# One core, three chained layers: a second PSUM tile for the last stage, its first block inside the last unit, and its rows loaded earlier

## The chip, the core and the metric

The kernel runs on one core of a Trainium2 chip. The core's engines each run their own list of instructions in order and wait for each other through semaphores: TensorE (PE in the profile, with PEld for its weight loads), VectorE (DVE), ScalarE (ACT), GpSimd (POOL), and SyncE (SP), which here issues nearly all DMA transfers. The metric is the time of one execution on the device in microseconds (us). Three runs of the kernel before took 1320.35, 1321.07 and 1323.45 us; the median is 1321.07.

## What is computed

The reference chains three layers over 4608 tokens of 512 numbers (batch 8, 8 heads, 576 positions, 64 per head). Cut to what matters:

```python
# 1. linear attention with random features
phi(x) = concat(exp(x @ w_phi - m), exp(-(x @ w_phi - m))),  m = max|x @ w_phi|
x = (phi(q) @ (phi(k).T @ v)) / (phi(q) @ sum(phi(k)))
# 2. mixture of 8 experts: each token goes to the expert with the largest logit
logits = x @ w_gate + modality_bias[modality_id]
out[mask_e] = gate_w * (relu(x[mask_e] @ w1[e]) @ w2[e])     # 512 -> 1024 -> 512
# 3. dense layer with a SoLU
h = x @ w_in                                                  # 512 -> 1024
solu = h * softmax(h)
ln = (solu - mean) / sqrt(var + 1e-6) * g_ln
result = ln @ w_out                                           # 1024 -> 512
```

## The kernel before

Products are made in a format that rounds, so each operand is split into a high and a low part and each product is three matmuls: high by high, high by low, low by high. `mm3` (L1071) issues the three, and its line, L1074, stands at almost every matmul below.

*Attention* fills the first 440 us; the change does not touch it. At its end the tokens lie in HBM (`xe`), sorted by expert.

*The experts* follow as units. Unit 0 has 128 rows; units 1 to 17 have 256 each (pairs); unit 18, the last (NU - 1), has 128 again; then come four *minis* of 32 rows, each of another expert. A pair unit runs `mm1` (four blocks of 24 matmuls of 256 columns, each block into one PSUM tile `tp`, read by ScalarE, L1088, and VectorE, L1089, in `relu_split`), in the midst of it eight transposes for the next unit's rows (`xT`, L898), and `mm2` (96 matmuls). The tile `tp` comes from the pool `bank` of 6 PSUM banks (L964). In `mm2` of a pair unit the two halves of the output have a `tp` each; half 0 is complete after step 2 of 4, half 1 after step 3, and each is copied (`yo`, L1188) and sent to HBM (`yd`, L1152) when it is complete. For the single unit 18 `mm1` keeps rows on partitions, so its result is turned by eight transposes (`tr_single`, L1108), which is put off in the list `mids` and run by `run_mids`. Weights come through eight buffers (ldk, ldq, ldv in the trace) that SP fills again as soon as they have been split; in unit 18 it fills them with weights of the minis.

The minis are a generator, `quad` (L1341): each `next(minis)` does one step of it (load rows; transpose; four steps of 32 small matmuls at L1357; transpose; four steps at L1373; copy; transpose and four stores to `yd`, L1386). 

*The last stage* works on 36 tiles of 128 tokens. `load_y(j)` loads two tiles' rows from `yd` into the SBUF buffer `yin` (L1210). Its address in `yd` is fixed, but units store at addresses held in registers, so it waits until every store issued before it has landed. `yT(i)` (L1216) splits a tile into high (`yTh`, ScalarE, L925) and low (`yTl`, GpSimd, L926). `a3(i)` (L1234) makes `h` by 24 matmuls of 512 columns into one PSUM tile of two banks (named `h2` in the code, `h` in the profile; pool `hps`, one buffer, L965), then the softmax and the norm: two maxima (DVE, L1244), the exponential (ACT, L1249), the product (DVE, L1254, the last that reads `h`), the centring (DVE, L1256), the squares (ACT, L1259). `turn` (L1224) has VectorE transpose the result in blocks of 32 (L1226) and sends it through HBM (`turned`, L1228, and `wlo`, L1232) to finish the transpose; `lnT` (L1272) splits what comes back (ACT L1281, DVE L1282); `a4(i)` (L1285) is the second product, 24 matmuls of 512 columns, and stores the rows.

`block()` (L1459) puts these together: in block n it issues `yT(n+1)`, `load_y` where n is even, `a3(n)`, `lnT(n-2)` and `a4(n-3)`. So the first three blocks have an `a3` and no `a4`. The order of issue is the order of the code on PE; after the units the other engines' orders come from a scheduler that follows the code closely. `units` (L1482) issues `load_y(0)` just before unit 18, but after the stores of unit 17, and `yT(0)` after unit 18. In unit 18 (L1405) the first two steps of the minis that use PE are issued between `mm1` and `mm2`. After the units, L1499 alternates one step of the minis with two blocks.

Of the kernel before, what the change touches and what calls it, by code (L numbers as in the profile page):

```python
# [17 lines left out]
P = 128  # L18
# [936 lines left out]
def moe(ctx, m):  # L955
# [5 lines left out]
    p2 = ctx.enter_context(tc.tile_pool(name="m_2", bufs=2, reuse_waits="tile"))  # L961
    p1 = ctx.enter_context(tc.tile_pool(name="m_1", bufs=1, reuse_waits="tile"))
    wp = ctx.enter_context(tc.tile_pool(name="m_w", bufs=1, reuse_waits="tile"))
    bank = ctx.enter_context(tc.tile_pool(name="m_b", bufs=6, space=PSUM, reuse_waits="tile"))  # L964
    hps = ctx.enter_context(tc.tile_pool(name="m_h", bufs=1, space=PSUM, reuse_waits="tile"))  # L965
    KD, KF = DM // P, DFF // P
    NU = 2 + NUNIT
    m.rp, m.xin = rp, p1
# [5 lines left out]
    def weights():  # L974
        gl = p1.tile([P, KF], F32, name="gl")
        SP.dma_start(out=gl, in_=m.g_ln.rearrange("(c p) -> p c", p=P))
        n = 2 * KD + KF
        tiles = {}

        def load(i):  # L980
            if i < 2 * KD:
                rows, c0 = m.w_in[(i // 2) * P : (i // 2 + 1) * P, :], (i % 2) * 512
            else:
                rows, c0 = m.w_out[(i - 2 * KD) * P : (i - 2 * KD + 1) * P, :], 0
            tiles[i] = p1.tile([P, 512, 2], I32, name=("yin", "ex")[i % 2])
            SP.dma_start(out=tiles[i], in_=rows[:, c0 : c0 + 512].bitcast(I32).rearrange("p (n two) -> p n two", two=2))

        load(0)
        yield
        for i in range(n):  # L990
            if i + 1 < n:
                load(i + 1)
            src = tiles.pop(i)
            h, l = src[:, :, 1], src[:, :, 0]
            ab = p1.tile([P, 2, 512], I32, name="wab")
            a, b = ab[:, 0, :], ab[:, 1, :]
            V.tensor_scalar(out=a, in0=h, scalar1=3, scalar2=0x3FFFFFF8, op0=ALU.logical_shift_left, op1=ALU.bitwise_and)
            V.scalar_tensor_tensor(out=b, in0=h, scalar=-0x40000000, in1=a, op0=ALU.bitwise_and, op1=ALU.bitwise_or)
            yield
            V.tensor_scalar(out=a, in0=b, scalar1=-0x800000, scalar2=None, op0=ALU.bitwise_and)  # L1000
            V.tensor_scalar(out=l, in0=l, scalar1=9, scalar2=None, op0=ALU.logical_shift_right)
            yield
            a, b = a.bitcast(F32), b.bitcast(F32)
            V.scalar_tensor_tensor(out=a, in0=l, scalar=2.0**-43, in1=a, op0=ALU.mult, op1=ALU.mult)
            V.tensor_tensor(out=a, in0=a, in1=b, op=ALU.add)
            V.tensor_scalar(out=h, in0=h, scalar1=0x7FF00000, scalar2=None, op0=ALU.bitwise_and)
            yield
            V.scalar_tensor_tensor(out=b, in0=h, scalar=float(897 << 20), in1=a, op0=ALU.is_ge, op1=ALU.mult)
            if i < 2 * KD:
                hi, lo = [t[:, (i % 2) * 512 : (i % 2 + 1) * 512] for t in win[i // 2]]  # L1010
                m.split(b, hi, lo, V)
            else:
                f = i - 2 * KD
                hi, lo = [t[:, f % 2, :] for t in wout[f // 2]]
                A.mul(hi, b, gl[:, f : f + 1])
                V.scalar_tensor_tensor(
                    out=lo, in0=b, scalar=gl[:, f : f + 1], in1=hi.bitcast(F32), op0=ALU.mult, op1=ALU.subtract
                )
            yield
# [70 lines left out]
        return hi, lo  # L1090

    def tr(src, nms, pool):
        hi, lo = [pool.tile([P, DFF], F32R, name=nm).rearrange("p (k t) -> p k t", k=KF) for nm in nms]
        for b0 in range(0, KF, 4):
            tp = bank.tile([P, 4, P], F32, name="tp")
            for j in range(4):
                T.transpose(tp[:, j, :], src[:, (b0 + j) * P : (b0 + j + 1) * P], c.ident)
            m.evac(hi[:, b0 : b0 + 4, :], lo[:, b0 : b0 + 4, :], tp)
        return hi, lo
# [50 lines left out]
    def put(o, u, n, dc):  # L1150
        rows = yd[dc * P : (dc + 4 // n) * P, m.cols(u)]
        SP.dma_start(out=rows.rearrange("(c p) t -> p c t", p=P), in_=o)  # L1152
# [15 lines left out]
    def mm2(us):  # L1168
        acc = {}
        for j in range(4):  # L1170
            fh, dh = j // 2, j % 2
            ch = (us[-1], 4 + j)
            w = chunks.pop(ch)
            for u in us:
                h = hT[u]
                if m.size(u) == 2:
                    if fh == 0:
                        acc[u, dh] = bank.tile([P, 2, 2 * P], F32, name="tp")
                    o = acc[u, dh]
                    for dc in range(2):  # L1180
                        for f in range(4):
                            mm3(
                                o[:, dc, :], both(w, lambda t: t[:, f, dc * P : (dc + 1) * P]), h(4 * fh + f),
                                fh == dc == f == 0, fh == 1 and f == 3,
                            )
                    if fh == 1:
                        yo = p2.tile([P, 2, 2 * P], F32, name="yo")
                        A.copy(yo, o)  # L1188
                        put(yo, u, 2, 2 * dh)
                else:  # L1190
                    if j == 0:
                        acc[u] = bank.tile([P, 2, 2 * P], F32, name="tp")
                    o = acc[u]
                    for f in range(4):
                        mm3(o[:, dh, :], h(4 * fh + f), both(w, lambda t: t[:, f, :]), j == f == 0, fh == 1 and f == 3)
                    if j == 3:
                        put_rows(o, u)
            used(ch)
            yield
        slots[0] += sum(m.size(u) for u in us)  # L1200
# [5 lines left out]
    def load_y(j):  # L1206
        assert 2 * j + 2 <= slots[0] - (NEW + 2 * NPAIR + NSING + 1 - NT), (j, slots)
        c0 = YCOLS - 2 * P * (j + 1)
        t = p1.tile([P, 4, 2 * P], F32, name="yin")
        SP.dma_start(out=t, in_=yd[:, c0 : c0 + 2 * P].rearrange("(c p) t -> p c t", p=P))  # L1210
        g = p2.tile([P, 2, 2], F32, name="gt", bufs=5)
        SP.dma_start(out=g, in_=gd[c0 : c0 + 2 * P, :].rearrange("(t p) w -> p t w", p=P))
        for n in range(2):
            ys[2 * j + n] = (t[:, :, (1 - n) * P : (2 - n) * P], g[:, 1 - n, 0:1], g[:, 1 - n, 1:2])
# [17 lines left out]
            SP.dma_start(out=lv[g], in_=dv[g])  # L1232

    def a3(i):  # L1234
        h = hps.tile([P, DFF], F32, name="h2")
        y = yt.pop(i)
        sc = lambda nm: p2.tile([P, 1], F32, name="s_" + nm)
        halves = [slice(n * 512, (n + 1) * 512) for n in range(2)]
# [69 lines left out]
    def extra(j):  # L1308
# [2 lines left out]
        e, xo = regs[u][:2]  # L1311
        for i in range(8):
            m.load_raw(i, e)
        x = p1.tile([P, DFF], F32, name="yin")[:, 0:DM]
        SP.dma_start(out=x, in_=m.xe[bass.ds(xo, P), 0:DM])
        m.keep_gates(u)

# [23 lines left out]
    def quad():  # L1341
# [40 lines left out]
        A.copy(yr, b.rearrange("p a d -> p (a d)"))  # L1382
        yield
        yo = blocks(yr, KD, [p2.tile([P, 4, P], F32, name="yo")])[0]
        for g, u in enumerate(us):
            SP.dma_start(  # L1386
                out=yd[:, m.cols(u)].rearrange("(c p) t -> p c t", p=P), in_=yo[:, :, group(g)]
            )
        slots[0] += 1
        yield  # L1390

    def run(g):
# [12 lines left out]
    def unit(u):  # L1405
        gap(u)
        g = mm1(u)
        for i in range(4):
            next(g)
            if i == XAT:  # L1410
                run_mids()
                next_x(u)
                if u == NU - 2:
                    next(minis)
        run(g)
        gap(u)
        if u == NU - 1:
            next(minis)
        run_mids()
        if u == NU - 1:  # L1420
            next(minis)
        run(mm2([u]))

    with ExitStack() as sp:
# [30 lines left out]
    mids.extend(held)  # L1455
    ctx.enter_context(tc.manual_schedule(engines={mybir.EngineType.SP}))
    nxt = [0, 0, 0]

    def block():  # L1459
        n, split, done4 = nxt  # L1460
        run_mids()
        if n + 1 < NT:
            yT(n + 1)
            if n % 2 == 0 and n + 2 < NT:
                load_y((n + 2) // 2)
        if n == NT - 1:
            lnT(split)
        if n < NT:
            a3(n)
            nxt[0] += 1  # L1470
        if split < n - 1:
            if n < NT - 1:
                lnT(split)
            nxt[1] += 1
        if done4 < n - 2:
            a4(done4)
            nxt[2] += 1
# [4 lines left out]

    def units(u0, u1):
        for u in range(u0, u1):
            if u == START - 1:
                run(bg)
                load_y(0)
            unit(u)
            if u == START - 1:
                yT(0)  # L1490

    minis = quad()
    with tc.manual_schedule(engines=MANUAL):
# [2 lines left out]
    if ENDMAN:  # L1496
        ctx.enter_context(tc.manual_schedule(engines=MANUAL))
    with tc.manual_schedule(engines=QMAN):
        for _ in minis:  # L1499
            block()  # L1500
            block()
# [76 lines left out]
```

## Time and profile before

| | us |
|---|---|
| median of three runs | 1321.07 |
| the profiled execution | 1319.59 |
| its span on the core | 1317.5 |
| PE busy in the span | 1270.6 (96%) |
| granted TensorE clock, mean | 0.988 |
| the last matmul ends, from the span's start | 1302.86 |

The span goes from the first instruction to the last; 2.1 us of the execution lie around it. The profile lists for each engine the groups of instructions with their busy time, and for each wait what ended it. A matmul of 512 columns is shown as 0.39 us long, but matmuls are pipelined and one starts every 0.23 us; the length of a run of them is read from the chain of waits, which merges them. [...]

### The profile page before, as it was taken

Reading aid. Unit: us, or ns where it says so; the run is one execution under the profiler, and the core shown is the slowest. Engines: PE = TensorE matmul, PEld = TensorE weight load, DVE = VectorE, ACT = ScalarE, POOL = GpSimd, SP = SyncE. Lnnn points to the kernel's source line nnn. Section 1 sums busy time; section 2 is a strip of 40 time slices with the busy share of each in tenths; the row PEclk is TensorE's granted clock in tenths of the full one; section 3 lists DMA queues with packets and bytes.
Section 4 is the critical chain, followed back from the end, with each engine's and each line's share of the span. In section 5 each row is a group of like instructions: output and inputs, shape, how many; then the busy total and the mean of one; then the engine's idle time right before and its main releaser. Section 6 shows DMA issues by size and latency. Waiting matters only on the chain.

```text
span 1317.5 us, 25489 instructions
## 1 busy us (share of the span) xinstructions
PE 1270.6 (96%) x9242; PEld 1064.4 (81%) x9242; DVE 865.9 (66%) x1620; ACT 668.2 (51%) x1254; POOL 409.8 (31%) x479
## 2 busy tenths in 40 slices
PE   8999999999999989999999999987999998999997
PEld 6777777777775989999999999855877787888885
DVE  7758867866885758777877878625555554555561
ACT  5666666666664345554555555513333443444442
POOL 6655665674672100000000000012233233333331
PEclk9999999999999999999999999988999998999998
DMA  8712421241132232215322221786767555556552
GB/s 241 209 53 64 132 96 57 92 143 49 50 130 81 74 91 67 79 59 171 94 81 66 81 81 26 231 258 166 200 188 202 137 132 131 139 131 151 136 136 56
DMA packets 273762, 156.81 MB, mean 119 GB/s; under 512 B 181824, under 2 KB 255712, under 8 KB 273632
## 3 DMA queue, kind: packets, MB, share of 16 engines
q1 hardware_dynamic: 267648, 136.01, 37.9%
q0 software_dynamic: 5824, 19.04, 3.8%
q8 instruction: 76, 1.25, 0.4%
q14 instruction: 54, 0.44, 0.1%
q10 hardware_dynamic: 160, 0.07, 0.0%
HBM read 166.67 MB, written 51.37 MB: 165 GB/s over the span
## 4 chain that ended last, share of the span: by engine, by line
PE 56%; DMA 3%; DVE 2%; issue 1%; ACT 1%; SPq 1%; POOLq 0%; ACTq 0%; DVEq 0%
PE tp L1074 39%; PE h L1074 14%; DMA yd<-yo 2%; PE tp L898 1%; DMA ldv<-in_moe_w_dram 1%; PE tp L1373 1%; ACT ex L1249 0%; DVE ex L1254 0%; DVE wlo L926 0%; PE tp L1357 0%; DMA yin<-yd 0%; SPq L1232 0%; DVE s_mx L1244 0%; DMA out_dram<-wab,gt 0%; DMA turned<-whi 0%
## 5 line engine op out<-in xcount | busy, mean ns | idle before, releaser
L322 POOL TENSOR_TENSOR es<-es,e 128x512 f32<-128x512 f32 x128 | 164.0, 1288 | 102.0 <-ACT e L278 90.4
L926 POOL TENSOR_TENSOR yTl<-yin,yTh 128x512 fp32r<-128x512 f32 x36 | 46.9, 1302 | 451.3 <-ACT yTh L925 447.6
L1244 DVE TENSOR_REDUCE s_mx<-h 128x1 f32<-128x512 f32 x72 | 46.4, 687 | 125.4 <-PE h L1074 125.4
L1074 PE MATMUL tp<-xTh,whi 128*128 128x256 f32 x432 | 122.4, 283 | 2.4 <-PEq L1443 2.4
L1074 PE MATMUL tp<-xTh,wlo 128*128 128x256 f32 x432 | 121.5, 281 | 0.0
L1074 PE MATMUL tp<-xTl,whi 128*128 128x256 f32 x432 | 121.3, 281 | 0.0
L1074 PE MATMUL tp<-hTl,whi 128*128 128x256 f32 x432 | 119.7, 277 | 0.4 <-DVE hTl L1089 0.4
L1074 PE MATMUL tp<-hTh,wlo 128*128 128x256 f32 x432 | 119.6, 277 | 0.3 <-DVE wlo L926 0.3
L1074 PE MATMUL tp<-hTh,whi 128*128 128x256 f32 x432 | 119.5, 277 | 0.0
L1249 ACT ACTIVATE ex<-h,s_mx,gt 128x1024 f32<-128x1024 f32 x36 | 43.4, 1207 | 136.0 <-issue 78.3
L271 DVE TENSOR_REDUCE m<-mm 128x4 f32<-128x512 f32 x144 | 97.1, 680 | 15.9 <-PE mm L269 15.9
L259 DVE TENSOR_TENSOR lo<-tp,hi 128x512 fp32r<-128x512 f32 x72 | 49.5, 687 | 81.8 <-ACT hi L258 81.3
L267 PE MATMUL mm<-wphi_hi,hi 128*128 128x256 f32 x288 | 93.8, 326 | 1.1 <-ACT hi L258 1.1
L1259 ACT ACTIVATE sq<-ex 128x1024 bf16<-128x1024 f32 x36 | 38.1, 1058 | 97.8 <-DVE ex L1256 97.8
L1262 POOL TENSOR_SCALAR rs<-s_var,gt 128x1 f32<-128x1 f32 x36 | 12.4, 344 | 236.3 <-ACT sq L1259 236.3
L1074 PEld LDWEIGHTS tp<-xTh,whi 128*128 128x128 f32 x432 | 82.1, 190 | 2.6 <-ACTq L1443 2.6
L338 ACT ACTIVATE qp<-tp 128x512 f32<-128x512 f32 x128 | 69.4, 597 | 25.8 <-PE tp L330 22.7
L1074 PEld LDWEIGHTS tp<-xTl,whi 128*128 128x128 f32 x432 | 81.9, 190 | 0.0
L1074 PEld LDWEIGHTS tp<-xTh,wlo 128*128 128x128 f32 x432 | 81.9, 190 | 0.0
L1074 PEld LDWEIGHTS tp<-hTl,whi 128*128 128x128 f32 x432 | 81.1, 188 | 0.6 <-DVE hTl L1089 0.6
L1074 PEld LDWEIGHTS tp<-hTh,wlo 128*128 128x128 f32 x432 | 81.1, 188 | 0.5 <-DVE wlo L926 0.5
L1074 PEld LDWEIGHTS tp<-hTh,whi 128*128 128x128 f32 x432 | 81.2, 188 | 0.0
(427 smaller groups left out, 3904.9 us busy)
## 6 DMA issues: line engine op xcount, KB each, us to landing
ldk<-in_moe_w_dram SPq DMA_DIRECT2D x66, 512.0 KB
ldv<-in_moe_w_dram SPq DMA_DIRECT2D x66, 512.0 KB
ldq<-in_moe_w_dram SPq DMA_DIRECT2D x44, 512.0 KB
turned<-whi SPq DMA_DIRECT2D x35, 512.0 KB
wlo<-turned SPq DMA_DIRECT2D x140, 128.0 KB
yd<-yo SPq DMA_DIRECT2D x36, 256.0 KB
yin<-yd SPq DMA_DIRECT2D x18, 512.0 KB
xin<-xe SPq DMA_DIRECT2D x16, 512.0 KB
```

The costliest lines, as they stand in the source:

```text
L259: V.tensor_tensor(out=lo, in0=tp, in1=hi.bitcast(F32), op=ALU.subtract)
L267: T.matmul(o, lhsT=hi[:, 2 * a + j, :], rhs=c.wphi_hi, start=(j == 0), stop=False, skip_group_check=True)
L271: V.tensor_reduce(out=m, in_=pj, axis=AX.X, op=ALU.max, apply_absolute_value=True)
L322: G.tensor_tensor(out=eo, in0=eo, in1=ev[:, :, r, :], op=ALU.add)
L338: A.activation(u.qp[half][:, fh, 2 * hp : 2 * hp + 2, o : o + 2 * P], tp.rearrange("p (h r) t -> p h (r t)", r=2), AF.Exp, scale=sc,)
L898: self.tc.nc.tensor.transpose(tp[:, k, :], x[:, t, k * P : (k + 1) * P], self.c.ident)
L926: eng.tensor_tensor(out=lo, in0=src, in1=hi.bitcast(F32), op=ALU.subtract)
L1074: T.matmul(o, lhsT=l, rhs=r, start=first and n == 0, stop=last and n == 2, skip_group_check=True)
L1244: V.tensor_reduce(out=mx, in_=h[:, sl], axis=AX.X, op=ALU.max, negate=True)
L1249: A.activation(ex, h, AF.Exp, bias=mx, scale=g, accum_out=sm)
L1259: A.activation(sq, ex, AF.Square, accum_out=var)
L1373: T.matmul(b[group(g), dh, :], lhsT=ht[fh][:, f, group(g)], rhs=m.w1c(j % 2 * NMINI + g)[:, f, :], start=j == f == 0, stop=fh == 1 and f = ...
```

## The change

There are five edits. (1) The pool `bank` goes from 6 PSUM banks to 4, and `hps` from one tile of two banks to two tiles; together they still fill the 8 banks. (2) `mm2` of a pair unit takes one tile of `hps` for both halves in place of two tiles `tp`, and both halves are copied and stored after its last step. (3) `yin` gets two buffers. `load_y(0)` moves from before unit 18 to the middle of unit 17, behind its `mm1` and so ahead of its stores; `load_y(1)` to block 0; and from there the load of tiles n+3 and n+4 is issued in block n where n is odd, a block sooner than before. (4) `yT(0)` and block 0 move into unit 18, between its `mm1` and its `mm2`; block 1 stands behind unit 18, then the first step of the minis with expert weights, then block 2, and then the alternation as before. The step of the minis that stood between `mm1` and `mm2` is thereby two blocks later. (5) The four stores of the minis are no longer issued together: each is put on a list, and blocks with an even number that load nothing issue one each.

```diff
-    bank = ctx.enter_context(tc.tile_pool(name="m_b", bufs=6, space=PSUM, reuse_waits="tile"))
-    hps = ctx.enter_context(tc.tile_pool(name="m_h", bufs=1, space=PSUM, reuse_waits="tile"))
+    bank = ctx.enter_context(tc.tile_pool(name="m_b", bufs=4, space=PSUM, reuse_waits="tile"))
+    hps = ctx.enter_context(tc.tile_pool(name="m_h", bufs=2, space=PSUM, reuse_waits="tile"))
...
                 if m.size(u) == 2:
-                    if fh == 0:
-                        acc[u, dh] = bank.tile([P, 2, 2 * P], F32, name="tp")
-                    o = acc[u, dh]
+                    if j == 0:
+                        acc[u] = hps.tile([P, 2, 2, 2 * P], F32, name="h2")
+                    o = acc[u][:, dh]
...
-                    if fh == 1:
-                        yo = p2.tile([P, 2, 2 * P], F32, name="yo")
-                        A.copy(yo, o)
-                        put(yo, u, 2, 2 * dh)
+                    if j == 3:
+                        for n in range(2):
+                            yo = p2.tile([P, 2, 2 * P], F32, name="yo")
+                            A.copy(yo, acc[u][:, n])
+                            put(yo, u, 2, 2 * n)
...
-        t = p1.tile([P, 4, 2 * P], F32, name="yin")
+        t = p1.tile([P, 4, 2 * P], F32, name="yin", bufs=2)
...
-        for g, u in enumerate(us):
+
+        def store(g, u):
             SP.dma_start(
                 out=yd[:, m.cols(u)].rearrange("(c p) t -> p c t", p=P), in_=yo[:, :, group(g)]
             )
-        slots[0] += 1
+            slots[0] += g == NMINI - 1
+
+        stores.extend(lambda g=g, u=u: store(g, u) for g, u in enumerate(us))
         yield
...
         run(g)
         gap(u)
+        if u == NU - 2:
+            run(bg)
+            load_y(0)
         if u == NU - 1:
             next(minis)
+            run_mids()
+            yT(0)
+            block()
         run_mids()
-        if u == NU - 1:
-            next(minis)
         run(mm2([u]))
...
             yT(n + 1)
-            if n % 2 == 0 and n + 2 < NT:
-                load_y((n + 2) // 2)
+            if n == 0:
+                load_y(1)
+            elif n % 2 and n + 3 < NT:
+                load_y((n + 3) // 2)
+            elif stores:
+                stores.pop(0)()
...
-            if u == START - 1:
-                run(bg)
-                load_y(0)
             unit(u)
-            if u == START - 1:
-                yT(0)
...
     with tc.manual_schedule(engines=QMAN):
+        held = mids[:]
+        mids.clear()
+        block()
+        mids.extend(held)
+        next(minis)
+        block()
         for _ in minis:
             block()
             block()
```

What this does to the orders shows at two places. On PE, at the end of the `mm1` of unit 18, before: transposes of the minis' rows (tp<-ident,xin), those of unit 18 (tp<-ident,ldq), and then the minis' first weights (ldk, ldq, ldv).

```order
L1304 MATMUL tp<-ident,xin 128x128 x4
L1108 MATMUL tp<-ident,ldq 128x128 x8
L1357 MATMUL tp<-ldk,xTh 32x256
L1357 MATMUL tp<-ldq,xTh 32x256
L1357 MATMUL tp<-ldv,xTh 32x256
```

And in the changed kernel, where h_12826 is the `h` of tile 0 and h_12946 that of tile 1:

```order
L1308 MATMUL tp<-ident,xin 128x128 x4
L1111 MATMUL tp<-ident,ldq 128x128 x8
L1074 MATMUL h_12826<-win0h,yTh 128x512
L1074 MATMUL h_12826<-win0l,yTh 128x512
L1074 MATMUL h_12946<-win0h,yTh 128x512
L1074 MATMUL h_12946<-win0l,yTh 128x512
L1074 MATMUL h_12826<-win0h,yTl 128x512
L1074 MATMUL h_12826<-win1h,yTh 128x512
```

The 24 matmuls of tile 0 stand where the minis stood (with two of tile 1 drawn forward); behind them come the 48 of unit 18's `mm2`, the other 22 of tile 1, the minis' 32, four transposes, tile 2, again 32 of the minis, tile 3 and the first `a4`.

On ACT, at the same place, before: the split of unit 18's turned rows (hTh), the copy of unit 18's output (yr), and then a split of a tile's rows (yTh) ahead of each exponential (ex).

```order
L887 CAST hTh_12813<-tp 128x512
L887 CAST hTh_12822<-tp 128x512
L1156 COPY yr<-tp 128x512
L925 CAST yTh<-yin 128x512
L1364 ACTIVATE ldq<-tp 128x512
L1163 COPY yo<-tp 128x512
L925 CAST yTh<-yin 128x512
L1249 ACTIVATE ex,s_sm<-h_12949,s_mx_12951,gt 128x1024
```

And in the changed kernel:

```order
L887 CAST hTh_12796<-tp 128x512
L887 CAST hTh_12805<-tp 128x512
L925 CAST yTh<-yin 128x512 x3
L1253 ACTIVATE ex,s_sm<-h_12826,s_mx_12828,gt 128x1024
L1263 ACTIVATE sq,s_var<-ex 128x1024
L1159 COPY yr<-tp 128x512
L1253 ACTIVATE ex,s_sm<-h_12946,s_mx_12948,gt 128x1024
```

Three tiles' rows are split ahead of the first exponential, the third of them from the second `load_y`, and the copy of unit 18's output stands behind the first tile's squares.

## Rows read from the trace of the kernel before

**Rows 1.** Windows: stretch, length, busy us of PE, PEld, DVE, ACT, POOL; clock, DMA, GB/s.

```profile
600.00:700.00 100.00, 99.62 (x858) 99.35 (x857) 78.97 (x103) 56.13 (x77) 0.00 (x0) 1.00 0.37 112
700.00:850.00 150.00, 150.00 (x1297) 150.00 (x1296) 113.68 (x145) 82.22 (x110) 0.00 (x0) 1.00 0.31 88
850.00:870.00 20.00, 15.21 (x129) 10.07 (x128) 3.62 (x5) 4.33 (x8) 1.27 (x1) 0.91 1.01 329
870.00:915.00 45.00, 32.45 (x146) 24.79 (x145) 18.75 (x36) 12.82 (x22) 9.52 (x16) 0.89 0.68 194
915.00:1075.00 160.00, 160.00 (x813) 125.93 (x812) 89.20 (x164) 63.55 (x112) 54.38 (x80) 1.00 0.67 172
1075.00:1120.00 45.00, 41.30 (x171) 33.15 (x170) 22.05 (x40) 15.58 (x28) 16.22 (x22) 0.92 0.58 132
```

**Rows 2.** Waits of PE from 840 us on: who for whom, total us, times, longest.

```profile
PE h L1074 <- DVE ex L1254: 16.2, 4, 4.8
```

**Rows 3.** Chain of waits, in order of time: start us, length us, what.

```profile
665.20 5.69 PE tp L1074 x48
...
848.37 7.32 DMA yd<-yo
...
869.67 0.59 PE tp L1161 x4
870.26 5.51 PE h L1074 x24
...
880.52 7.24 PE h L1074 x24
...
904.72 7.09 PE h L1074 x24
911.81 5.60 PE tp L1074 x24
917.41 1.86 PE tp L1357 x32
...
930.59 5.50 PE h L1074 x24
...
1103.02 3.66 DMA yin<-yd
...
1107.28 1.30 ACT ex L1249 x2
...
1110.43 8.25 PE h L1074 x24
```

**Rows 4.** Timeline of PE, unit 18 into the minis: start, length, what [idle before, releaser].

```profile
850.34 1.07 PE L1108 MATMUL tp<-ident,ldq 128*128 128x128 f32 x8
...
857.09 0.64 PE L1357 MATMUL tp<-ldk,xTh 128*32 128x256 f32 x2 [1.44 <-DMA ldk<-in_moe_w_dram]
```

**Rows 5.** Timeline of all engines, a tile's rows split behind unit 18's.

```profile
852.01 1.08 ACT L887 CAST hTh<-tp 128x512 fp32r<-128x512 f32 x2
...
866.74 0.62 ACT L925 CAST yTh<-yin 128x512 fp32r<-128x512 f32 x1
...
867.44 1.27 POOL L926 TENSOR_TENSOR yTl<-yin,yTh 128x512 fp32r<-128x512 f32 x1 [429.86 <-ACT yTh L925]
```

**Rows 6.** Timeline of SP, the load that the minis waited for at 857.09.

```profile
849.97 0.37 SPq L884 DMA_DIRECT2D ldk<-in_moe_w_dram  x1
```

**Rows 7.** Timeline of DVE, the split ahead of the first `a4`.

```profile
907.27 1.33 DVE L1282 TENSOR_TENSOR wlo<-wlo,whi 128x512 fp32r<-128x512 f32 x2 [0.50 <-ACT whi L1281]
```

**Rows 8.** Timeline of SP, the minis' four stores.

```profile
1091.92 9.29 SPq L1386 DMA_DIRECT2D yd<-yo  x4
```

**Rows 9.** Timeline of all engines in the pair unit with the least slack.

```profile
567.00 0.59 ACT L1188 COPY yo<-tp 128x512 f32<-128x512 f32 x1
...
570.78 0.68 DVE L1089 SCALAR_TENSOR_TENSOR hTl<-tp,hTh 128x512 fp32r<-128x512 f32 x1
...
572.13 0.36 PE L1074 MATMUL tp<-xTh,whi 128*128 128x256 f32 x1
```

More of the change, by code (lines that the diff above doesn't have):

```diff
@@ L984, in load @@
                 rows, c0 = m.w_out[(i - 2 * KD) * P : (i - 2 * KD + 1) * P, :], 0
-            tiles[i] = p1.tile([P, 512, 2], I32, name=("yin", "ex")[i % 2])
+            tiles[i] = p1.tile([P, 512, 2], I32, name=("yin", "ex")[i % 2], bufs=2 - i % 2)
             SP.dma_start(out=tiles[i], in_=rows[:, c0 : c0 + 512].bitcast(I32).rearrange("p (n two) -> p n two", two=2))
@@ L1092, in tr @@
     def tr(src, nms, pool):
-        hi, lo = [pool.tile([P, DFF], F32R, name=nm).rearrange("p (k t) -> p k t", k=KF) for nm in nms]
+        hi, lo = [
+            pool.tile([P, DFF], F32R, name=nm, **({"bufs": 2} if nm == "yin" else {})).rearrange("p (k t) -> p k t", k=KF)
+            for nm in nms
+        ]
         for b0 in range(0, KF, 4):
@@ L1234, in a3 @@
     def a3(i):
-        h = hps.tile([P, DFF], F32, name="h2")
+        h = hps.tile([P, 2, 2, 2 * P], F32, name="h2").rearrange("p a b t -> p (a b t)")
         y = yt.pop(i)
@@ L1313, in extra @@
             m.load_raw(i, e)
-        x = p1.tile([P, DFF], F32, name="yin")[:, 0:DM]
+        x = p1.tile([P, DFF], F32, name="yin", bufs=2)[:, 0:DM]
         SP.dma_start(out=x, in_=m.xe[bass.ds(xo, P), 0:DM])
@@ L1457, in moe @@
     nxt = [0, 0, 0]
+    stores = []
     def block():
```

## The prediction

> **What bounds the kernel now.** I read the windows by stage first. From 700 to 850 us and from 915 to 1075 us TensorE is busy all the time at a clock of 1.00; only 850 to 870, 870 to 915 and 1075 to 1120 show it idle (4.8, 12.5 and 3.7 us) and at clocks of 0.91, 0.89 and 0.92 [rows 1]. So outside these places only fewer or shorter matmuls would help, and the change has the same matmuls. Then the waits of PE: behind 840 us, 16.2 us in four waits for the product at L1254, the last that reads the single tile `h` [rows 2]. Last the chain, which puts them in order [rows 3]: three of the four stand between the `a3` of tiles 0 to 3, where no `a4` exists yet to fill the time; the fourth stands ahead of 1110.43. In 850 to 870 the waits are for the minis' weights (1.44 us at 857.09) [rows 4]: `load_y(0)` stood on SP until the stores of unit 17 had landed (7.32 us from 848.37 [rows 3]), with weight loads behind it.
>
> **The clock.** [...] I charge 1.74 us for a wait of some us (7.24 - 5.50); the rows bound it by 0 and 2.75 us (8.25 - 5.50).
>
> **The beginning of the last stage.** The transposes of unit 18 end at 850.34 + 1.07 = 851.41 [rows 4], in both kernels alike; the first `a4` ends at 911.81 + 5.60 = 917.41 [rows 3]. Both kernels do the same work between these points. It took 66.0 us. At full clock it is: `mm2` of unit 18, 48 matmuls of 256 columns, 5.69; two steps of the minis, 2 x 1.86; four transposes, 0.59; four `a3`, 4 x 5.50; one `a4`, 5.60 [rows 3]. Together 37.6 us, so 28.4 us were waits and slow clock. What is late in the changed order:
>
> - Tile 0 follows unit 18's transposes at once, and needs its split. ACT ends unit 18's split at 852.01 + 1.08 = 853.09 [rows 5]; the first of unit 17's two copies now stands with the second, behind its `mm2`, which may shift this by one copy, 0.59 us [rows 9]. Then `yTh` 0.62, and `yTl`, which began 0.08 us behind it and takes 1.27 [rows 5]: 855.65 at the latest. PE is free from 851.41 and has four matmuls of 0.23 us (5.50 / 24) that need only `yTh`. It idles 4.24 - 0.92 = 3.3 us, or 2.7 without the shift. I take 3.3, and the charge of 1.74 for the clock, since the waits of 3.7 and 4.8 us were followed by the lower clock.
> - The rows for tile 0 must be there by 853.7. `load_y(0)` now stands ahead of three weight loads and both stores of unit 17, at about 844, and nothing that it waits for is young (the stores of unit 16 are a unit old). A load of the same 512 KB took 7.1 us in the busiest part (849.97 [rows 6] to 857.09 [rows 4]). It lands by 852: no cost.
> - `a3(1)` has the second tile, `a3(2)` comes 5.69 + 22 x 0.23 + 1.86 + 0.59 = 13 us after `a3(0)`, and tile 0 is released 4.7 us after its last matmul (870.26 + 5.51 to 880.52 [rows 3]). No wait, and 8 us of cover: it holds as long as the exponential of tile 0 is not 8 us late. `a3(3)` comes 1.86 us after `a3(2)`, into the other tile.
> - `a4(0)` has less time: only 1.86 + 5.50 = 7.36 us lie between the end of `a3(2)` and it. Before, `a3(2)` ended 4.8 us [rows 2] ahead of 904.72, at 899.9, and the second half of the split for `a4(0)` ended at 907.27 + 1.33 = 908.60, the first at about 907.94 [rows 7]: 8.0 and 8.7 us. PE waits 0.6 us; bounds 0 and 1.3.
>
> 28.4 - 3.3 - 1.7 - 0.6 = 22.8 us gained here.
>
> **The minis' stores.** Before, the four stores stood together on SP for 9.29 us, each until the one before had landed [rows 8], and `load_y` behind them: its rows came at 1103.02 + 3.66, the exponential of tile 19 stood on ACT behind the split of these rows and began at 1107.28, and PE waited 3.70 us for `h` and then ran at the lower clock [rows 1, 3]. With a store every second block (some 22 us) each has landed before the next, and the load is a block sooner. The gain is 3.70 + 2.75 = 6.45 us. Should a single store still hold a load, it is for some 2.3 us (a quarter of 9.29) beside 11 us of matmuls per block; no cost.
>
> **Four banks in the pair units.** In a pair unit the third block of `mm1` now takes the bank of the first, and so waits until VectorE has split that. I looked through 15 of the 16 units, from 500 us on, for the least slack: the split ended at 570.78 + 0.68 = 571.46 and the third block began at 572.13 [rows 9], 0.67 us later. The copy that now stands before it on ACT costs 0.59 us there, and in this unit VectorE, not ACT, was late. So nothing; bounds 0 and 0.6 us in each of 16 units.
>
> **The rest.** Copies and stores are as many as before; a store of unit 17 goes out up to 3 us later, and the loads that wait for it no longer hold weights that PE needs. Steady blocks have PE busy all the time [rows 1] and the same PE work, so the second tile saves nothing there.
>
> **The sum.** 22.8 + 6.45 = 29.2 us. The profiled execution took 1319.59 us, so 1290.4 for it; the median of the runs lies 1.48 us above it, and I predict 1292. With the small bounds (no clock charge, a start wait of 2.7, no wait at `a4(0)`: 32.1 us) 1289, and 1287 if the run is like the profiled one; with the large ones (clock charge 2.75, 1.3 us at `a4(0)`, 3 us in the units) 1297.
>
> **Rivals.**
>
> - *The second tile brings little, because something else is late at the same place* (about 1301). ACT, in order, has the exponential of tile 0 behind the split of tile 2, whose rows come by the second `load_y`, which on SP stands behind five weight loads and waits for unit 17's stores. If it is issued only when these stores have landed (848.37 + 7.32 = 855.69) and one more load (7.1) is through, and takes 7.1 itself, it lands at 869.9, while tile 0's product ends near 862.5 (855.65 + 22 x 0.23 + 1.74); unit 18's output copy behind it, and the transposes and `a3(2)` behind that, come some 3 to 5 us late, with another 1.74 for the clock, and `a3(3)` after them. For it speaks that this very order on ACT made the wait at 1110.43; against it that these stores are issued before the five loads and landed in 7.3 us. The price without any use of the second tile: in the new order a single one would cost 4.7 - (1.86 + 0.59) = 2.3 us ahead of `a3(2)` and 4.7 - 1.86 = 2.9 ahead of `a3(3)`, and 1.74 each for the clock: 8.7 us, 1292 + 8.7 = 1300.7. [...]
> - *Only the stores pay* (1321.07 - 6.45 = 1314.6). The beginning would then lose as much in new places as it saves, 22.8 us; I find only the 5.6 us above.
> - *Slower: four banks make PE wait in every pair unit, and each wait costs clock as well* (about 1328). With w us of wait in 16 units and 1.74 us of clock each, the price is 16 x (w + 1.74); at w = 0.6 (one copy) 37 us, against 29.2 gained: 8 us slower. It decides from w = 0.1 on if every such wait lowers the clock, and from 1.8 us on if none does. Against it: the slack of at least 0.67 us [rows 9], and that 0.38 us of idle in 600 to 700 left the clock at 1.00 [rows 1]. [...]
>
> **How the numbers follow.** The forecast gets 0.70 (its own range 1287 to 1297), the first rival 0.16, only the stores 0.04, the slower one 0.06, and 0.04 is for no net change by several of these. The range 1286 to 1304 takes in the forecast and the first rival. A difference under 0.3% (4 us) can't be told from none here. Faster by more: 0.70 + 0.16 + 0.04 = 0.90; the same 0.04; slower 0.06.
>
> **What would show it.** In the profile after, the last matmul ends near 1274 us of the span and not 1302.86; PE's waits for `h` from L1254 are gone or under 2 us in all; one wait of 2.5 to 3.5 us for the split of tile 0 stands behind unit 18's transposes, with one stretch of lower clock; no stretch of lower clock at the minis' stores; no waits of PE for VectorE at L1089 in the units. If waits of PE for L1089 appear all over 490 to 840 us, the bank edit was mis-sized; if the exponential of tile 0 begins after 868 us, the first rival holds.

## The result, and the profile after

| | before | after |
|---|---|---|
| median, same chip | 1322.26 us (4 runs) | 1298.82 us (4 runs) |
| the profiled execution | 1319.59 us | 1298.82 us |
| mean granted clock | 0.988 | 0.994 |

The ratio is 0.9819 (95% interval 0.9804 to 0.9833). Timed again on another chip it was 0.9806 (0.9793 to 0.9820; 1304.02 against 1328.91 us). So the change gains 23 to 25 us; forecast were 29.2.

The windows of the kernel after, in the columns of [rows 1]; the clock is the share of full speed that TensorE was granted:

```profile
850.00:870.00 20.00, 16.20 (x90) 14.02 (x89) 8.56 (x10) 7.21 (x11) 2.51 (x2) 0.83 1.03 335
870.00:915.00 45.00, 44.95 (x278) 34.16 (x277) 28.72 (x53) 20.11 (x35) 13.59 (x25) 1.00 0.62 167
...
1075.00:1120.00 45.00, 45.00 (x199) 36.57 (x198) 26.26 (x48) 19.26 (x34) 16.36 (x25) 1.00 0.61 141
```

From 870 to 915 us TensorE (PE) was idle for 12.5 us before and for 0.05 now; from 1075 to 1120 it was idle for 3.7 and now not at all. Both stretches have the full clock (1.00, and 0.89 and 0.92 before). The idle time that is left, and the lower clock (0.83), stand in 850 to 870. PE's waits from 440 us on, as in [rows 2] (who for whom, total us, times, longest):

```profile
PE tp L1074 <- DVE hTl L1089: 2.6, 1, 2.6
PE h L1074 <- ACT yTh L925: 2.3, 1, 2.3
PE tp L1074 <- ACTq L1454: 2.2, 1, 2.2
PE tp L1111 <- ACT ldq L1144: 1.5, 1, 1.5
PE tp L1074 <- ACT whi L1285: 0.6, 1, 0.6
...
```

The 16.2 us for the product behind the exponential (L1254, now L1258) are gone. The first row is new, and it lies in unit 2, 370 us ahead of the last stage; the third is a branch (L1454) for which ScalarE, VectorE and SyncE wait too (3.1, 1.9 and 4.3 us), and in the kernel before it cost PE 2.4 us. The chain after, in the columns of [rows 3]:

```profile
847.18 6.88 DMA ldk<-in_moe_w_dram
...
854.14 1.04 ACT whi L925
855.19 0.42 ACT ldq L1144
...
858.16 0.53 ACT yTh L925
...
858.73 8.73 PE h L1074 x26
867.46 5.68 PE tp L1074 x48
873.14 5.07 PE h L1074 x22
...
897.06 9.24 DMA turned<-whi
...
914.57 8.83 DMA turned<-whi
...
930.31 6.13 PE tp L1074 x24
...
1114.65 5.50 PE h L1074 x24
...
1276.52 5.60 PE tp L1074 x24
```

The first `a3` runs in one piece with `mm2` and the next `a3`. Its first 26 matmuls take 8.73 us at a granted clock of 0.69, where 26 x 5.50 / 24 = 5.96 would be full speed. The `a3` that took 8.25 us at the minis' stores has its like in the 5.50 of 1114.65. The last PE piece of the chain ends at 1276.52 + 5.60 = 1282.12 us, 20.74 sooner than before; forecast was 1274. (PE's records go on behind this piece in both kernels, to 1287.71 after and 1308.44 before; that "the last matmul" ends at 1302.86 was imprecise, the difference is the same.)

The prediction named a sign for its first rival: the exponential of tile 0 begins after 868 us. It did, at 872.30 (in a trace in which the units end 3.3 us later than in that of the kernel before):

```profile
871.77 0.62 ACT L925 CAST yTh<-yin 128x512 fp32r<-128x512 f32 x1 [12.58 <-DMA yin<-yd]
872.30 1.21 ACT L1253 ACTIVATE ex<-h,s_mx,gt 128x1024 f32<-128x1024 f32 x1
...
874.01 1.28 DVE L1258 SCALAR_TENSOR_TENSOR ex<-ex,s_r,h 128x1024 f32<-128x1024 f32 x1
```

ScalarE (ACT) had the split of tile 2 ahead of it, and that waited for the rows of the second `load_y`, as the rival said; the maxima that the exponential needs were there at 869.04. Tile 0's `h` was free at 875.30, and `a3(2)`, which takes it, began at 880.40 without a wait.

**A measure for the experiments.** Chips and runs differ by some us ahead of unit 2, where no trace shows a wait that the edits make: the cast of unit 2's first weights (`whi<-ldq`, 480.01 in the trace after) began between 478.4 and 489.5 us in the fourteen traces. So beside the ratio I give the tail of each profiled run, from that cast to the end of PE's records: 1308.44 - 478.43 = 830.01 us before, 1287.71 - 480.01 = 807.70 after. The profile's own gain of 20.77 us is thus 22.3 in the tail less 1.6 ahead of it. The tail falls into two parts at the first transposes of the minis' rows, near the end of unit 18, before and after:

```profile
849.90 0.60 PE L1304 MATMUL tp<-ident,xin 128*128 128x128 f32 x4
```

```profile
853.24 0.60 PE L1308 MATMUL tp<-ident,xin 128*128 128x128 f32 x4
```

From the cast to there, the units, it is 371.47 us before and 373.23 after; from there on, the last stage, 458.54 and 434.47. So the last stage gained 24.1 us, and the units, by the wait in unit 2, gave back 1.8. One profile settles no difference of some 2 us: the same changed kernel, profiled again, has 374.89 and 432.16, with a granted clock of 0.83 in the ten us around the end of unit 2's wait (490 to 500), where the first profile has 1.00 (481 to 491), and of 0.91 in the 20 us around the start of the last stage (859 to 879), where the first has 0.83 (850 to 870).

| kernel | median us | before, same chip | ratio (95% interval) | tail us |
|---|---|---|---|---|
| before | | | 1 | 830.01 |
| after | 1298.82 | 1322.26 | 0.9819 (0.9804 to 0.9833) | 807.70 |
| after, again | 1304.02 | 1328.91 | 0.9806 (0.9793 to 0.9820) | 807.05 |
| one tile | 1311.03 | 1327.38 | 0.9871 (0.9845 to 0.9897) | 817.00 |
| tiles only | 1319.87 | 1327.38 | 0.9945 (0.9926 to 0.9963) | 818.49 |
| stores only | 1321.19 | 1327.38 | 0.9953 (0.9933 to 0.9972) | 824.48 |
| stores together | 1305.02 | 1327.38 | 0.9830 (0.9801 to 0.9859) | 809.90 |
| bank of unit 2 | 1302.68 | 1329.70 | 0.9801 (0.9772 to 0.9830) | 804.73 |
| gates spread | 1302.31 | 1329.70 | 0.9798 (0.9769 to 0.9828) | 808.32 |
| one row buffer | 1317.99 | 1329.70 | 0.9906 (0.9880 to 0.9933) | 823.94 |
| block 0 behind | 1305.00 | 1329.70 | 0.9815 (0.9790 to 0.9841) | 805.06 |
| bank and gates | 1299.78 | 1328.91 | 0.9781 (0.9768 to 0.9794) | 802.71 |
| bank and block | 1301.11 | 1328.91 | 0.9779 (0.9759 to 0.9798) | 804.82 |
| all three | 1303.62 | 1328.91 | 0.9803 (0.9788 to 0.9817) | 805.85 |

### The profile page after: what moved, and what is told of

It is laid out like the page before. It is cut to its first block, busy times and chain, and to the rows that moved or that the text cites. A ratio compares the mean times of both kernels' runs of the same rounds, so it can differ in the third digit from the quotient of the medians.

```text
span 1296.8 us, 25369 instructions
## 1 busy us (share of the span) xinstructions
PE 1263.6 (97%) x9242; PEld 1060.2 (82%) x9242; DVE 866.1 (67%) x1620; ACT 666.7 (51%) x1254; POOL 403.4 (31%) x479
## 4 chain that ended last, share of the span: by engine, by line
PE 55%; DMA 4%; DVE 1%; ACT 1%; issue 1%; SPq 0%; POOLq 0%; ACTq 0%; DVEq 0%
PE tp L1074 27%; PE h L1074 26%; DMA turned<-whi 2%; PE tp L898 1%; DMA wlo<-turned 1%; DMA gd<-xe 1%; PE tp L1377 1%; DMA ldk<-in_moe_w_dram 1%; ACT whi L925 0%; SPq L1236 0%; DVE wlo L926 0%; DMA out_dram<-wab,gt 0%; DVE s_mx L1248 0%; DVE wlo L1286 0%; PE tp L1361 0%
## 5 line engine op out<-in xcount | busy, mean ns | idle before, releaser
L1074 PE MATMUL h<-hTl,whi 128*128 128x256 f32 x432 | 119.6, 277 | 0.4 <-DVE hTl L1089 0.4
L1074 PE MATMUL h<-hTh,wlo 128*128 128x256 f32 x432 | 119.4, 276 | 0.0
L1074 PE MATMUL h<-hTh,whi 128*128 128x256 f32 x432 | 119.4, 276 | 0.0
L1074 PEld LDWEIGHTS h<-hTl,whi 128*128 128x128 f32 x432 | 81.1, 188 | 0.6 <-DVE hTl L1089 0.6
L268 PE MATMUL mm<-wphi_lo,hi 128*128 128x256 f32 x288 | 81.4, 283 | 0.0
L269 PE MATMUL mm<-wphi_hi,lo 128*128 128x256 f32 x288 | 81.2, 282 | 0.0
L1074 PEld LDWEIGHTS h<-hTh,whi 128*128 128x128 f32 x432 | 81.2, 188 | 0.0
```

Source lines behind the costliest of these rows:

```text
L268: T.matmul(o, lhsT=hi[:, 2 * a + j, :], rhs=c.wphi_lo, start=False, stop=False, skip_group_check=True)
L269: T.matmul(o, lhsT=lo[:, 2 * a + j, :], rhs=c.wphi_hi, start=False, stop=True, skip_group_check=True)
L1074: T.matmul(o, lhsT=l, rhs=r, start=first and n == 0, stop=last and n == 2, skip_group_check=True)
```

## The experiments

The theory: the second tile and the rows a block ahead take away the four waits; four banks cost a wait in one unit; the rest of the gap to the forecast lies at the start of the last stage. The rival is the first one of the prediction, in which the tile brings little. "-" lines are the changed kernel's, unless said otherwise.

**One tile.**

```diff
-    bank = ... bufs=4 ...;  hps = ... bufs=2 ...
+    bank = ... bufs=6 ...;  hps = ... bufs=1 ...
-                        acc[u] = hps.tile([P, 2, 2, 2 * P], F32, name="h2")
+                        acc[u, dh] = bank.tile([P, 2, 2 * P], F32, name="tp")
...
```

> The changed kernel with its PSUM edits undone: six banks, one tile h, mm2's accumulators in banks; the first block in unit 18, the row loads and the spread stores stay. Theory (the second tile pays at the start of the last stage, and four banks cost one wait in unit 2): a3(2) waits about 2.3 us for the exponential and a3(3) about 2.9 us, each with up to 1.7 us of lower clock, 5 to 9 us lost; the wait of 2.6 us at the transposes of unit 2 is gone, 2.3 us won. Together 3 to 7 us slower than the changed kernel, so 1302 to 1306. Rival (the second tile brings little, because other things are late at the same place): within 2 us of the changed kernel, or faster by the 2.3 us of unit 2.

By the ratios 0.9871 - 0.9819 = 0.52% slower than the changed kernel, some 7 us; by the tails 9.3. PE's waits:

```profile
PE h L1074 <- DVE ex L1257: 7.8, 3, 3.0
...
PE tp L1074 <- DVE hTl L1089: 0.4, 1, 0.4
```

The waits for the exponential are back, three and not two (2.6, 2.3 and 3.0 us), and the wait of unit 2 is gone. The one that I had not expected stands ahead of `a3(1)`: the exponential of tile 0 began at 873.43, again behind the split of tile 2. So the second tile pays, and its banks also make the wait in unit 2: against the kernel after, the last stage is 11.6 us longer and the units are 2.3 shorter. The size is at the upper end of what I expected by the ratios, and above it by the tails; the rival is out.

**Tiles only** ("-" is the kernel before).

```diff
-    bank = ... bufs=6 ...;  hps = ... bufs=1 ...
+    bank = ... bufs=4 ...;  hps = ... bufs=2 ...
...
```

> The kernel before with the PSUM edits alone: four banks, two tiles, mm2's accumulators in a tile; order, rows and stores as before. Theory (the second tile removes the early waits, but the rows that come a block ahead then hold the third and fourth block): of the waits of 3.7 to 4.8 us on L1254 at the start the three go or shrink, 8 to 12 us won with some of the clock, a wait for rows of some 2 us remains, the wait at the minis' stores stays, and unit 2 costs 2.3 us: 5 to 12 us faster than before, 1310 to 1317. Rival (the order and the loads do it all, the tile nothing): within 2 us of before, or 2.3 us slower.

A gain of 0.55%, 7.3 us, as expected (11.5 in the tail; the profiled run was the fastest of six). PE's waits:

```profile
PE h L1074 <- ACT yTh L925: 3.9, 2, 2.3
...
PE h L1074 <- POOL yTl L926: 1.9, 3, 0.6
PE tp L1074 <- ACT whi L1282: 1.8, 1, 1.8
PE tp L1074 <- DVE hTl L1089: 1.7, 1, 1.7
```

None is left for the exponential, but `a3(2)` now waits 2.3 us for its rows, the minis' stores still cost 1.6 us for theirs (both in the first row; 3.7 us before), and the first `a4` waits 1.8 us. The tile takes the waits for `h` away and the rows are next.

**Stores only** ("-" is the kernel before).

```diff
-        for g, u in enumerate(us):
+        def store(g, u):
...
+        stores.extend(lambda g=g, u=u: store(g, u) for g, u in enumerate(us))
...
+            elif stores:
+                stores.pop(0)()
```

> The kernel before with the spread stores of the minis alone. Theory (the sum's own term): the wait of 3.70 us at the minis' stores and the 2.75 us of lower clock behind it go, 6.45 us faster than before, about 1315.8. Rival (a single store still holds the load of the rows): the wait stays in part, 0 to 3 us faster.

A gain of 0.47%, 6.2 us; 5.5 in the tail. Of the four waits for the exponential three are left:

```profile
PE h L1074 <- DVE ex L1254: 12.5, 3, 4.8
```

12.5 = 16.2 - 3.7: the one at the minis' stores went, as the sum had it, and its price of 6.45 us was about right.

**Stores together.**

```diff
-        def store(g, u):
+        for g, u in enumerate(us):
```

> The changed kernel with the minis' four stores put together again, in one step. Theory: the 9.29 us on SP hold the row load behind them, but with a load ahead into a second buffer the rows are wanted a block (11 us) later, so most of the wait is covered: 0 to 2 us slower than the changed kernel. Rival (the stores' term belongs to the spread stores alone): 6.45 us slower, about 1305.

0.11% slower than the changed kernel (1.5 us, the intervals overlap); the tail is 2.2 us longer, of which 1.5 lie in the units and 0.7 in the last stage. (Unit 2's wait is 4.2 us here against 2.6, but in both it ends 2.96 us after the cast; the clock behind it was 0.83 here, in 485 to 495, and 1.00 there.) From 1000 to 1140 us PE does not stop:

```profile
1000.00:1140.00 140.00, 140.00 (x679) 111.23 (x678) 78.75 (x144) 56.18 (x99) 48.53 (x72) 1.00 0.66 166
```

The rows a block ahead cover the stores. So the 6.45 us do not belong to the spread stores alone: with one tile and the late loads the spread stores bring them, and with two tiles and the early loads they bring almost nothing. (The tile has a part in this: with the tiles only, the wait of 3.7 us there was 1.6. Early loads with one tile and the stores together were not tried.)

**One row buffer.**

```diff
-            if n == 0:
-                load_y(1)
-            elif n % 2 and n + 3 < NT:
-                load_y((n + 3) // 2)
+            if n % 2 == 0 and n + 2 < NT:
+                load_y((n + 2) // 2)
```

with one buffer `yin`. 

> The changed kernel with one buffer for the rows and the loads in the even blocks, as before the change. Theory (the rows of a block were there in time except where something held SP): 0 to 1 us slower in the steady blocks, and the rows of tiles 2 and 3, which a store or unit 17's weights can hold, up to 3 us: 0 to 4 us slower. Rival (loading ahead into two buffers is what lets a3(2) go without a wait): over 5 us slower.

The rival's size held, and by far: 0.87% slower, some 12 us (16.2 in the tail, 14.7 of it in the last stage; of its six runs the profiled one was the slowest). Its place did not: `a3(2)` has no wait, and the longest, 7.9 us, stands ahead of `a3(4)`. PE's waits, then the chain and SP's queue around the longest:

```profile
PE h L1074 <- ACT yTh L925: 12.1, 4, 7.9
```

```profile
901.91 8.32 DMA yd<-yo
910.28 3.96 DMA yin<-yd
...
```

```profile
898.50 0.82 SPq L884 DMA_DIRECT2D ldk<-in_moe_w_dram  x1
...
901.30 0.37 SPq L884 DMA_DIRECT2D ldk<-in_moe_w_dram  x1
901.91 0.40 SPq L1155 DMA_DIRECT2D yd<-yo  x1
910.28 0.38 SPq L1214 DMA_DIRECT2D yin<-yd  x1
```

The load of tiles 4 and 5 stands on SP behind four weight loads of the minis and a store of unit 18, and goes out at 910.28, when that store has landed. In the changed kernel it goes out at 883.28 (below), ahead of both, 21 us sooner as counted from the cast. (The experiment moves the load as well as the buffer; one buffer does not allow the earlier load, so the two were not tried apart.)

```profile
883.28 0.97 SPq L1214 DMA_DIRECT2D yin<-yd  x1
```

**The bank of unit 2.**

```diff
-            tp = bank.tile([P, 4, P], F32, name="tp")
+            if u:
+                tp = bank.tile([P, 4, P], F32, name="tp")
+            else:
+                tp = hps.tile([P, 2, 2, 2 * P], F32, name="h2")[:, 0].rearrange(...)
```

> The changed kernel, in which unit 0's output transposes take a half of an h tile instead of a bank, so that the third block of unit 2 waits for the split of the block two before it, as in the other units. Theory (one more tile in the rotation of four banks makes the wait of 2.60 us in unit 2): the wait falls to 0.3 us or less, 2.3 us faster than the changed kernel, about 1296.5. Rival (four banks are short there anyway, or the wait only moves to the next block): within 0.7 us of the changed kernel.

The wait of 2.6 us is 0.2 (below); by the ratios 0.18% faster than the changed kernel, 2.4 us, which the intervals alone would not settle; the tail is 3.0 us shorter, 1.7 of it in the units.

```profile
...
PE tp L1074 <- DVE hTl L1089: 0.2, 1, 0.2
```

What happens in unit 2 of the changed kernel, on its timeline:

```profile
480.01 1.05 ACT L925 CAST whi<-ldq 128x1024 fp32r<-128x1024 f32 x1 [3.12 <-SPq L1454]
480.96 0.59 ACT L1088 ACTIVATE hTh<-tp 128x512 fp32r<-128x512 f32 x1
481.09 1.23 DVE L926 TENSOR_TENSOR wlo<-ldq,whi 128x1024 fp32r<-128x1024 f32 x1 [3.47 <-ACT whi L925]
...
482.24 0.68 DVE L1089 SCALAR_TENSOR_TENSOR hTl<-tp,hTh 128x512 fp32r<-128x512 f32 x1
...
482.97 0.39 PE L1074 MATMUL tp<-xTh,w 128*128 128x256 f32 x1 [2.60 <-DVE hTl L1089]
```

The transposes of unit 0's output take a bank between the second block and the third, so the third block gets the bank of the block just before it. The split of that block stands on ACT and VectorE behind a cast of weights for which both waited some 3 us at the branch (L1454).

**The gates spread.**

```diff
-            m.keep_gates(u)
+            stores.append(lambda u=u: m.keep_gates(u))
```

> The changed kernel, in which the minis' gates go out one at a time, at every other block of the last stage, and not in a chain of four in unit 17. Theory (the chain of gate stores on SP makes the weight load late by which PE waits 1.47 us at the first transposes for the minis): the load is issued 4 us sooner or more, the wait goes, 1.5 us faster than the changed kernel, up to 3 with the clock: 1296 to 1297.5. Rival (the wait for tile 0's split ends at the same time anyway, or the gates hold a row load later): within 0.7 us, or slower.

The wait at L1111 is gone (the transposes there are unit 18's, not the minis'), but the one wait of an `a4` for its split is 2.0 us and not 0.6, at a later tile, and the tail is as long as before the edit (808.32). The ratio 0.9798 would mean 2.8 us, but its interval reaches to none. The new wait in the trace, PE's and the chain ahead of it:

```profile
983.37 0.66 PE L1074 MATMUL tp<-wout0h,whi 128*128 128x512 f32 x1 [2.04 <-ACT whi L1285]
```

```profile
967.98 8.73 DMA turned<-whi
```

That is the first leg of `turn`, by which a later block's result goes through HBM to be transposed. It took 8.73 us behind four weight loads and a row load, all issued in the 6 us before it; in the kernel after, at 885.10 with only a row load issued just before it, the same 512 KB took 4.38. The chain of gate stores did make the first wait; whether the edit alone pays stays open.

**Block 0 behind unit 18's second product.**

```diff
             yT(0)
-            block()
```

and one more `block()` behind unit 18. 

> The changed kernel with its first block behind unit 18's second product, and not in front of it; the transposes and the split of tile 0 stay in unit 18. Theory (the two waits of 1.5 and 2.3 us at the start go, since the second product, which needs nothing new, fills them, but a4(0) then has less before it): within 2 us of the changed kernel, sooner faster than slower. Rival (the first block inside the last unit is what pays, since the second product covers tile 0's exponential): 3 us slower or more, with a wait ahead of a4(0) or a3(2).

0.9815, the same as the changed kernel; the tail is 2.6 us shorter than in its first profile and 2.0 than in its second, which one profile does not settle. The two waits of 1.5 and 2.3 us went; 1.7 us for the split of unit 18's turned rows and 1.4 for tile 2's came. The rival is out: the place of the first block, the part that the change names, pays nothing by itself. The clock in 840 to 870 is the full one, 1.00:

```profile
840.00:870.00 30.00, 27.91 (x237) 27.41 (x236) 15.56 (x16) 15.92 (x22) 2.55 (x2) 1.00 0.77 222
```

**Versions, beside the changed kernel again.** They join the edits shown.

> The changed kernel again, unchanged, as the mark for the three versions timed beside it. Expected: a ratio of 0.9819 to before, within 0.003, and the same waits of TensorE behind 470 us (2.6 us in unit 2, 1.5 and 2.3 us at the start of the last stage, 0.6 us at its second second-product).

> The changed kernel with two edits: unit 0's output transposes in a half of an h tile, and the minis' gates one at a time at every other block. Theory (two separate waits): 2.3 us for the first, and for the second 1.5 us if the row transposes of the fourth block are not late, nothing if the loads crowd them again (2.0 us of wait, as in the run of the gates alone): 2 to 4 us faster than the changed kernel. Rival (each wait that goes comes back in the next place): within 1 us of it.

> The changed kernel with two edits: unit 0's output transposes in a half of an h tile, and the first block behind unit 18's second product. Theory: 2.3 us for the first, some 1.6 us for the second (no stretch of lower clock at the start, waits of 3.8 us there in all): 3 to 5 us faster than the changed kernel. Rival (the first block inside the last unit is worth something that one profile did not show): 0 to 2 us faster.

> The changed kernel with all three edits: unit 0's output transposes in a half of an h tile, the gates one at a time, the first block behind unit 18's second product. Theory: as the two of bank and block, and since the weights and rows come some 4 us sooner the waits for the split of unit 18's rows (1.7 us) and for the rows of tile 2 (1.4 us) shrink too: 4 to 7 us faster than the changed kernel. Rival (the row transposes that wait behind crowded loads eat it): 2 to 4 us faster.

The mark came out as expected, but with one wait of 3.0 us at the start in place of 1.5 and 2.3. Bank and gates is the fastest by the medians (by the ratios bank and block is level with it): 4.2 us below the mark, and its slowest run (1301.27) is below the mark's fastest (1302.79); the two intervals just touch. Its waits:

```profile
PE h L1074 <- ACT yTh L925: 2.3, 1, 2.3
...
PE tp L1074 <- ACT whi L1288: 0.6, 1, 0.6
```

Here the crowding cost 0.6 us, and the tail is 2.0 us shorter than with the bank alone; that the gates paid is likely and not settled. Bank and block gained 2.9 us by the medians and 3.6 by the ratios, about what I expected, but its interval overlaps the mark's. All three missed: 0.4 us by the medians, where 4 to 7 were expected. Its trace has three waits, of which bank and gates has only the second, and shorter:

```profile
PE h L1074 <- POOL yTl L926: 1.7, 2, 1.4
PE tp L1074 <- ACT whi L1288: 1.4, 2, 1.0
PE tp L1074 <- ACT hTh L887: 1.3, 1, 1.3
```

With block 0 behind, tile 2's split stands on ScalarE behind tile 0's squares, and its low half on GpSimd behind tile 0's norm; `a3(2)` begins at 883.58 and goes on with the low half at 885.63. All waits of PE behind the cast sum up to 5.4 us here and to 4.4 with bank and gates, which is 1 of the 3.1 us between the two tails. The rest is in the same places: the profile counts idle time from the end that it models for a matmul, and the wait of 1.0 us cost more than that: from start to start the `a3` ahead of it takes 6.99 us in place of 5.50. From the minis' transposes to the first step of the minis' second product it is 127.3 us with bank and gates and 130.3 here, at the full clock (1.00) in both.

## Why the forecast was right in kind and too large

The main reasons held: the waits for `h` went, one wait for tile 0's split came, the stores' wait went. The sum of 29.2 us came out as 22.3 in the tail, and the time, 1298.82 us, lies above the 1287 to 1297 that its own bounds gave. By its terms:

- *28.4 us of waits and slow clock at the start.* The step "both kernels do the same work between these points" failed. Up to the end of the first `a4` the kernel before did three steps of the minis, and I counted two (of the third, at 887.7, the chain shows nothing); the changed kernel does two. One step is 1.86 us, so the work is 39.5 us and the waits 26.5. (The wait at 857.09 was not `load_y(0)`'s doing, as the prediction has it: its load went out at 849.97, ahead of that. The load behind it is one issued at 859.44, for which PE waited 0.98 us at 867.76.)
- *The wait for tile 0's split, 3.3 us.* It came as 1.47 + 2.34 = 3.8 in two places, and as 3.0 in the other run. That unit 18's transposes end alike in both kernels did not hold: on ScalarE the result that they turn (L1144) stood behind the split of a weight of unit 18 (854.14), whose load SP issued only at 847.18, after four gate stores. The run with the gates spread shows it.
- *The clock, 1.74 us.* In the kernel before, the granted clock bears the charge out: it was 0.78 in the 7.24 us of the `a3` at 880.52 (0.50 up to 883.5), 0.80 in the 7.09 at 904.72 and 0.67 in the 8.25 at 1110.43, against 1.00 in the 5.50 at 930.59. In the kernel after it was 8.73 - 5.96 = 2.77 us, at the upper bound; with bank and gates a wait of 2.3 us at the same place left the clock at 1.00, so the term can also be nothing. What decides it stays open.
- *The second tile's cover, 8 us.* Some 3 of them were used, since the exponential of tile 0 was late as the first rival had it. The rival's cause came true and its price did not, so the sign that I had named for it, a start after 868 us, could not tell the two apart.
- *The wait at the first `a4`, 0.6 us.* No wait of PE is listed there, but its weight loads wait for the split (0.46 us for each half), and from its start (893.76) to the next (899.75) it takes 5.99 us in place of 5.60: 0.4. The fourth `a4` waited 0.6 us (930.31, 6.13 long, so 1.15 in all), behind the transposing stores of 9.24 and 8.83 us.
- *The stores, 6.45 us.* The size was right (6.2 alone), but I gave it to the spread stores; the earlier load, with the second tile, brings it as well.
- *Four banks, nothing.* The rival's mechanism was at work in one unit. The slack was read in 15 of 16 units, from 500 us on, and the one left out cost some 2 us (1.8 against the kernel before, 2.3 against one tile): there an extra tile shifts the rotation. In the other units the bound of no cost held: from 500 to 840 us PE is idle for 0.4 us in all, with six banks and with four.
- *The rows, nothing.* I priced their loads at no cost where they stand now, which is right, but did not see what they are worth: with the tile alone or with one buffer, PE waits for them next. The first rival's price for a single tile, 8.7 us, less the 2.3 us of unit 2, is 6.4; the run with one tile lost about 7, and in the profiles 11.6 less 2.3, with a third wait that the price leaves out.

Together 1.86 + 0.5 + 1.0 - 0.2 + 1.15 + 1.8 = 6.1 of the 6.9 us that lack; 0.8 stays unassigned.

## What to carry to other kernels

Parts of a change that remove waits in a row do not add up: the tiles alone gain 7 us, the stores alone 6, yet leaving out the tiles costs 7, the early rows 12, and the spread of the stores 1.5. Ask of each part what is late next, and count the work between two marks in both kernels, piece by piece, before waits are taken as a difference. When a pool gets fewer buffers, walk through all of its allocations: here one extra tile in one odd place made the third block of unit 2 wait 2.6 us for another predecessor.

## What the runs showed of the hardware

- The transposing store of 512 KB (`turned`) took 4.38 us with one load beside it and 8.73 to 9.24 us behind four weight loads and a row load or a store, and PE then waited for what it brought: 0.6 us at 930.31 behind the one that began at 914.57, and 2.0 us at 983.37 in the run with the gates spread.
- The same wait did not cost the same clock. A wait of 2.3 us ahead of tile 0 went with a granted clock of 0.94 in 840 to 870 us with the gates spread (the first line), and of 1.00 with bank and gates (the second):

```profile
840.00:870.00 30.00, 27.74 (x205) 25.91 (x204) 14.80 (x15) 15.79 (x22) 2.51 (x2) 0.94 0.90 281
840.00:870.00 30.00, 27.63 (x209) 25.76 (x209) 16.31 (x18) 16.82 (x24) 2.87 (x3) 1.00 0.82 253
```

- Small stores in a row held SP's queue for 11.8 us. In the kernel after, the four gate stores (0.2 KB each) with a load of a mini's rows ahead of each take SP from 834.65 to 846.4 us; on the chain three of them stand with

```profile
834.65 5.27 DMA gd<-xe
...
840.11 1.85 DMA gd<-xe
841.98 3.88 DMA gd<-xe
```
